# Two layers of local attention and SwiGLU: where staging and the size pass write, and in which order two attention streams run

## The chip, the cores and the metric

The kernel runs on one core of one Trainium2 chip. The metric is the device time of one execution in microseconds (us). Before the change it is 1657.15 us, the median of 18 runs (1651.94 to 1660.99). Engines are named as the profile names them: PE (matrix products; PEld is its weight load), DVE (VectorE), ACT (ScalarE), POOL (GpSimd) and SP (SyncE, which here issues nearly all DMAs).

## The reference, cut to what matters

One sequence of 2048 tokens, D = 1024, 32 heads of 32, F = 3584, in bf16. Two layers share one set of weights:

```
for layer in range(2):
    x = x + A(layernorm(x))     # attention
    x = x + B(layernorm(x))     # SwiGLU
A: q, k, v = split(x @ wqkv)
   each token attends to itself and to the tokens 2, 4, ..., 14 before it (W = 8)
   o = softmax(q . k[those] / sqrt(32)) . v[those];  return o @ wo
B: return (silu(x @ w1) * (x @ w3)) @ w2
```

## The kernel before, in words

**Units.** The tokens are cut into four chunks of 512. A unit is one layer's SwiGLU of one chunk; there are eight (`units`, L88). The stages on PE are: q, k and v of layer 0 for all four chunks (L956 to L973), then the eight units in turn (`b_stage`, L869). After the units 1 to 4 come q, k and v of layer 1 for the chunk that is three units ahead (L982 to L987). Attention runs beside these on DVE, in half chunks of 256 tokens (`halves`, L454).

**q, k, v.** `q_part` (L685) computes one of q, k, v for one chunk, transposed: 8 tiles of 8 matmuls (L699). ACT copies each result (L703) into a staging tile `sgt` of two tiles (pool `stg`, two buffers, L77), and SP stores it to a DRAM tensor `qkv_d` (L710). Attention later loads q, k and v of a half from there (`load_part`, L429). After each pair of tiles `then` may issue further loads (L714).

**Attention on DVE.** `score_steps` (L463) takes a half at a time. It multiplies q by eight shifted k (L478) and folds each product in a tree (L402, L404) into `psm`. PE sums over each head's elements (`gather_heads`, L491), DVE and ACT make the softmax (L508 to L522), and PE spreads it back over the partitions (`spread_heads`, L531), which ACT copies into `At` (L533). `value_steps` (L543) then multiplies `At` by shifted v (L562) and folds it into `oT`. `o_tile` (L633) multiplies `oT` by wo on PE (L649) and DVE adds the result to x (L654). Products of both streams take their buffers from the pool `scr` (three). In the kernel before, the score stream stops after queueing the spreading of half h until `At` of h is there (L540), so that the products of half h+1 begin no earlier than the values of h.

**Order.** The order on PE, DVE, ACT and SP is written out by a planner at build time (`manual_schedule`, L81). It keeps a modelled clock of each engine (`now`), with costs written by hand. `background(until)` (L130) puts steps of four queues, in the order norms, sums, values, scores, on DVE as long as they end before `until`. A step is a triple of cost, earliest time and action; a queue that yields `"blocked"` is passed over. PE's attention products wait in `pe_queue` and are put in when the modelled PE clock is 1.5 us past their due time (L457). `x_at` (L90) holds the modelled times at which the four chunks of x are there, `xnT_at` those of the normalised, transposed chunks. The normalisation has two parts, `norm_stats` (L203, DVE statistics L210) and `norm_apply` (L223), which writes `xn` (three buffers) and issues a transposing DMA on SP (L240).

**Weights.** All weights go through one ring of six slots of 8 KB per partition (pool `wp`). `seq` (L576) lists what the ring holds in order; `load_weight` (L591) fills the next entry, and `release`/`flush` (L622, L626) call it once for each slot that PE has finished with. SP issues these loads in program order with everything else.

**SwiGLU.** The units 0 and 1 (u < TU) work in groups of four tiles of 128 columns: w1 (L898, `pg`), Silu on ACT (L902), w3 (L907, `pu`), product on DVE (L911). A group is 64 matmuls. The columns are taken in two splits of four and three groups, and each split is followed by its w2 products (L924). At the side the units 0 and 1 prepare w1 and w3, one each, for the other six units, which form the products from seven combinations of quarter blocks (`products`, L775, matmuls L793). `prepare` (L758) does this by slots, two for each tile of the group. In slot 2, `measure` (L720) lets ACT take the sum of absolute values of the group's weights, the size pass (L723). In slot 5 a matmul sums it over the partitions (L729), DVE turns it into a scale (L733 to L736), and ACT copies the first half of the group, scaled, into block 0 of `big` (L744). In slot 6 ACT copies the second half into block 1. In slot 7 DVE forms the differences in block 0 (L754) and SP stores the block to `t_d` (L756); in slot 1 of the next group the same follows for block 1.

**The buffer `big`** (L183, 8192 elements of two bytes per partition) is used for several things: in the units 0 and 1 for the blocks 0 (from 0) and 1 (from 4096), and for the size pass's element-wise result, which nobody reads (0 to 4096, `junk`); in the later units for `sums` (0 to 3072) and five snapshots of partial products (`snaps`, 3072 to 8192).

Of the kernel before, what the change touches and what calls it, by code (L numbers as in the profile page):

```python
# [8 lines left out]
BF16 = mybir.dt.bfloat16  # L9
# [8 lines left out]
def kernel(  # L18
# [13 lines left out]
    nc = tc.nc  # L32
    cfg = dict(cfg or {})
    P = 128
# [34 lines left out]
    wp = ctx.enter_context(tc.tile_pool(name="wp", bufs=NW))  # L69
    xnp = ctx.enter_context(tc.tile_pool(name="xn", bufs=3))  # L70
    xtp = ctx.enter_context(tc.tile_pool(name="xnT", bufs=2))
    scr = ctx.enter_context(tc.tile_pool(name="scr", bufs=3))
    wk = ctx.enter_context(tc.tile_pool(name="wk", bufs=1))
    smp = ctx.enter_context(tc.tile_pool(name="smp", bufs=1))
    sgp = ctx.enter_context(tc.tile_pool(name="sg", bufs=5))
    small = ctx.enter_context(tc.tile_pool(name="small", bufs=2))
    stg = ctx.enter_context(tc.tile_pool(name="stg", bufs=2))  # L77
    qkvp = ctx.enter_context(tc.tile_pool(name="qkvp", bufs=1))
    dram = ctx.enter_context(tc.tile_pool(name="dram", bufs=1, space=DRAM))
    psum = ctx.enter_context(tc.tile_pool(name="psum", bufs=8, space=PSUM))  # L80
# [6 lines left out]
    now = dict(pe=23.6, dve=15.0, act=24.5, table=None)  # L87
    units = [(l, c) for l in range(2) for c in range(NCH)]  # L88
    norms = []
    x_at = [12.5, 21.5, 25.0, 28.5]  # L90
    xnT_at, norm_left, qkv_at, oT_at, o_todo = {}, {}, {}, {}, {}

    def pe(n, ready=0.0):
# [129 lines left out]
    def norm_apply(key, c, r):  # L223

        if key not in xnTs:
            xnTs[key] = xtp.tile([P, KT, CH], FP16, name="xnT")
        xnT = xnTs[key]
        mv, sd, ready = moments[key, r]
        rstd = small.tile([P, 2], FP32, name="rstd")

        def apply(i):
            j = 2 * r + i
            if key[0] == "Q" and key[1] == 0:
                xn = hT[:, KT + 2 * j:KT + 2 * j + 2, :].rearrange("p a t -> p (a t)").bitcast(FP16)
            else:
                xn = xnp.tile([P, D], FP16, name="xn")[:]
            nc.vector.tensor_scalar(xn, x_sb[:, c * TPC + j, :], mv[:, i, 0:1], rstd[:, i:i + 1],
                                    op0=ALU.subtract, op1=ALU.mult)
            with hp():
                nc.sync.dma_start_transpose(out=xnT[:, :, j * P:(j + 1) * P], in_=xn)  # L240
            xnT_at[key] = now["dve"] + DMA
            norm_left[key] = norm_left.get(key, TPC) - 1

        yield 0.10, ready, lambda: nc.vector.reciprocal(rstd[:], sd[:])
        for i in range(2):
            yield 0.47, 0.0, lambda: apply(i)

    moments = {}
    sums_of, sums_free = {}, [True]

# [26 lines left out]
    def first_q(ws, loads):  # L277
# [18 lines left out]
        load_tile(3, 0, D, nc.sync)  # L296
        load_weight()
        load_weight()
        for c in range(1, NCH):
            load_x(c)  # L300
        preload = small.tile([P, 1], FP32, name="preload", bufs=1)
        nc.scalar.activation(preload[:], epst[:], ACTF.Sqrt)

# [139 lines left out]
        qks[l, h] = qT, kT, max(now["dve"], qkv_at[l, h // R, 1]) + DMA  # L443

    def load_v(l, h):
        if (l, h) in vs or (l, h // R, 2) not in qkv_at or len(av_done) < len(vs):
            return
        vT = qkvp.tile([P, KT, HALO + TCH], BF16, name="vT")
        load_part(vT, l, 2, h * TCH, True)
        vs[l, h] = vT, max(now["dve"], qkv_at[l, h // R, 2]) + DMA  # L450
# [12 lines left out]
    def score_steps():  # L463

        V = nc.vector
        for g, (l, h) in enumerate(halves):
# [21 lines left out]
            def gather_heads(t):  # L488
# [3 lines left out]
                                     rhs=psm[:, :, a * BLK:(a + 1) * BLK], start=True, stop=True)  # L492
                at["t"] = pe(3, t) + 0.2

            t = now["dve"] + 0.2
            pe_queue.append((t, lambda: gather_heads(t)))
            while "t" not in at:
# [28 lines left out]
            At = Ats[l, h] = wk.tile([P, W, TCH], BF16, name="At")  # L526
            t2 = now["dve"] + 0.2

            def spread_heads(a):
                ps = psum.tile([P, W, BLK], FP32, name="pe", tag="mm")  # L530
                nc.tensor.matmul(ps[:], lhsT=spread[:, a, :], rhs=An[:], start=True, stop=True)  # L531
                r = pe(1, t2)
                nc.scalar.copy(At[:, :, a * BLK:(a + 1) * BLK], ps[:])  # L533
                done = act(0.6, r)
                if a == 3:
                    At_at[l, h] = done

            for a in range(4):
                pe_queue.append((t2, lambda a=a: spread_heads(a)))
            while (l, h) not in At_at:  # L540
                yield "blocked"

    def value_steps():  # L543

# [32 lines left out]
    for u in range(len(units)):  # L577
        for f0, f1 in fsplits:
            if u >= TU:
                groups = [(m, g0 // FG) for g0 in range(f0, f1, FG) for m in range(2)]  # L580
                for i, (m, g) in enumerate(groups):
                    seq += [("early", m, g)] + ([("late", *groups[i - 1])] if i else [])
                seq += [("late", *groups[-1])]
            for g0 in range(f0, f1, FG) if u < TU else ():
                seq += [("w1", g0, min(FG, f1 - g0)), ("w3", g0, min(FG, f1 - g0))]
            seq += [("w2", g0, min(8, f1 - g0), hh) for hh in range(2) for g0 in range(f0, f1, 8)]
        if 1 <= u and u + 3 < len(units):
            seq += [("qkv", which, h) for which in range(3) for h in range(2)]
    w_tiles, due, used = [], [], [0]

    def load_weight(pieces=1):  # L591

        if len(w_tiles) == len(seq):
            return
        kind, i, n, *rest = seq[len(w_tiles)]
        if kind == "qkv":
            w = wp.tile([P, KH, D], BF16, name="wqkv", tag="w")
            step = KH // pieces
            for k0 in range(0, KH, step):
                nc.sync.dma_start(w[:, k0:k0 + step, :],  # L600
                                  wqkv_v[:, n * KH + k0:n * KH + k0 + step, i * D:(i + 1) * D])
        elif kind in ("early", "late"):
            early = kind == "early"
            w = wp.tile([P, 2, 4 if early else 3, KT // 2, P], FP16, name=kind, tag="w")
            v = t_d[i][n][:].rearrange("p a (b k c) -> p a b k c", b=7, k=KT // 2)
            nc.sync.dma_start(w[:], v[:, :, 0:4] if early else v[:, :, 4:7])
        elif kind == "w2":
            w = wp.tile([P, 8, 512], BF16, name="w2t", tag="w")
            nc.sync.dma_start(w[:, 0:n, :], w2_v[:, i:i + n, rest[0] * 512:(rest[0] + 1) * 512])
        else:  # L610
            w = wp.tile([P, KT, FG * P], BF16, name=kind + "t", tag="w")
            v = w1_v if kind == "w1" else w3_v
            nc.sync.dma_start(w[:, :, 0:n * P], v[:, :, i * P:(i + n) * P])
        w_tiles.append(w)
# [7 lines left out]
    def release(n):  # L622

        due.extend([None] * n)
# [60 lines left out]
    def q_part(l, c, which, ws, then=()):  # L685
# [6 lines left out]
            kT = qkvp.tile([P, KT, HALO + TCH], BF16, name="kT")  # L692
            nc.vector.memset(kT[:, :, 0:HALO], 0.0)
        for t0 in range(0, KT, SG):
            sgt = stg.tile([P, SG, CH], BF16, name="sgt")
            for t in range(t0, t0 + SG):
                ps = bank("ps")
                for kk in range(KT):
                    nc.tensor.matmul(ps[:], lhsT=ws[kk // KH][:, kk % KH, t::KT], rhs=xnT[:, kk, :],  # L699
                                     start=(kk == 0), stop=(kk == KT - 1))  # L700
                r = pe(KT, ready)
                background(r)
                nc.scalar.copy(sgt[:, t - t0, :], ps[:])  # L703
                done = act(0.6, r)
                if first:
                    nc.scalar.copy(kT[:, t, HALO:], ps[:, 0:TCH])
                    done = act(0.4)
                if t < t0 + SG - 1:
                    pe_requests(2)
            nc.sync.dma_start(qkv_d[l][which][:, t0:t0 + SG, c * CH:(c + 1) * CH], sgt[:])  # L710
            if first and t0 == SG:
                load_part(qT, 0, 0, 0, False)
            between(False)
            if t0 // SG < len(then) and then[t0 // SG]:  # L714
                then[t0 // SG]()
# [1 line left out]
        if first:  # L717
            qks[0, 0] = qT, kT, done + 0.1

    def measure(m, g, w):  # L720

        junk = big[:, 0:4096].bitcast(BF16).rearrange("p (k c) -> p k c", k=KT)
        nc.scalar.activation(junk, w[:], ACTF.Abs, accum_out=size[:, m, g:g + 1])  # L723
        act(3.7)

    def scales(m, g):
# [28 lines left out]
        dve(1.4, r)  # L755
        nc.sync.dma_start(t_d[m][g][:, a, :], b.rearrange("p b k c -> p (b k c)"))  # L756

    def prepare(u, g, slot, w1t, w3t):  # L758

        w = (w1t, w3t)[u]  # L760
        if slot == 1 and g:
            differences(u, g - 1, 1)
        elif slot == 2:
            measure(u, g, w)
        elif slot == 5:
            scales(u, g)
            copies(u, g, w, 0)
        elif slot == 6:
            copies(u, g, w, 1)
        elif slot == 7:  # L770
            differences(u, g, 0)
            if g == NG - 1:
                differences(u, g, 1)
# [95 lines left out]
    def b_stage(u, hold):  # L869
# [7 lines left out]
        for (f0, f1) in fsplits:  # L877
# [4 lines left out]
                    sums_free[0] = True  # L882
            for g0 in range(f0, f1, FG) if u < TU else ():
                gn = min(FG, f1 - g0)
                w1t, w3t = weight("w1"), weight("w3")
                for fi in range(gn):
                    f = g0 + fi
                    slack = 1.0 if f < f1 - 2 else -0.5
# [12 lines left out]
                    sg = sgp.tile([P, CH], BF16, name="sg")  # L901
                    nc.scalar.activation(sg[:], pg[:], ACTF.Silu)  # L902
                    ts = act(0.6, r, "silu")
                    prepare(u, g0 // FG, 2 * fi, w1t, w3t)
                    pu = bank("pu")
                    for kk in range(KT):
                        nc.tensor.matmul(pu[:], lhsT=w3t[:, kk, fi * P:(fi + 1) * P], rhs=xnT[:, kk, :],  # L907
# [2 lines left out]
                    background(r + slack)  # L910
                    nc.vector.tensor_tensor(hT[:, f - f0, :], sg[:], pu[:], op=ALU.mult)  # L911
                    th = dve(0.64, r)
                    prepare(u, g0 // FG, 2 * fi + 1, w1t, w3t)
                release(2)
            for hh in range(2):
                w2ts = [weight("w2") for g0 in range(f0, f1, 8)]
                for j in range(TPC):
# [38 lines left out]
    for c in range(NCH):  # L956
        for which in range(3):
# [5 lines left out]
            if c == 0 and which == 0:  # L963
                continue
            if c == 0 and which == 1:
                then = (lambda: (load_weight(), load_weight()),)
            if c == 2 and which == 0:
                then = (None, None, lambda: nc.sync.dma_start(wo[:], wo_v))
            q_part(0, c, which, w_tiles[2 * which:2 * which + 2], then)
# [48 lines left out]
```

## Time and profile before

| | |
|---|---|
| time, median of 18 runs | 1657.15 us |
| time of the profiled execution | 1657.59 us |
| its span, first to last instruction | 1655.9 us |
| PE, busy | 1598.7 us |
| DVE, ACT, busy | 1223.2, 643.2 us |
| mean granted clock of PE | 0.981 |
| main DMA queue, share of 16 engines | 70.9% |
| stores of q, k, v (`qkv_d<-sgt`) | 92 of 256 KB, 2.3 us to landing |
| stores of blocks (`t_d<-big`) | 28 of 896 KB, 5.0 us to landing |
| loads of w1 and w3 for the units 0 and 1 | 14 and 14 of 1 MB, 7.0 and 8.8 us |
| size passes (L723) | 14 of 3.6 us on ACT |

The profile is of one execution. "Busy" is the time in which an engine has an instruction running. Lists of waits give the engine and line that stood idle, what ended the idle time, the total, the number of times and the longest. The chain of waits is followed back from the last instruction: at each step to what released it. The granted clock is the share of full speed at which PE was allowed to run.

### The profile page before, as it was taken

To read this page: it belongs to the slowest core of one execution; us is meant where nothing else is said; L and a number is where in the kernel's file an instruction comes from. 1 tells how busy PE (TensorE), PEld (TensorE's weight loads), DVE (VectorE), ACT (ScalarE), POOL (GpSimd) and SP (SyncE) were. 2 spreads that over 40 slices of the span, in tenths; PEclk is the share of its full clock that TensorE was granted. 3 is DMA by queue.
4 is the path that set the end of the run, shared out by engine and by line. 5 is a ranking of instruction groups with operands and counts; after the bars stand their busy time and mean duration, and the time that the engine had idled before them with its cause. 6 is when DMAs were issued, how large, how long until landed. Compare 5 with 4: busy or idle time off the path is not lost.

```text
span 1655.9 us, 24405 instructions
## 1 busy us (share of the span) xinstructions
PE 1598.7 (97%) x9844; PEld 1019.9 (62%) x9844; DVE 1223.2 (74%) x2180; ACT 643.2 (39%) x1000; POOL 3.4 (0%) x16
## 2 busy tenths in 40 slices
PE   9899999989899999999999999999999999999999
PEld 7565534434344468585685856857568577676866
DVE  6697687777786769888788978888769798734423
ACT  4433266354716336150452424514245225232422
POOL 0000000000000000000000000000000000000000
PEclk9999989999899999999999999999999999999999
DMA  9554766658766868776787778867779687677954
GB/s 310 161 135 123 207 192 207 197 187 269 229 196 194 282 198 296 228 246 213 233 264 232 255 221 286 255 207 258 214 251 266 231 274 237 226 248 249 322 181 147
DMA packets 298785, 377.90 MB, mean 228 GB/s; under 512 B 71472, under 2 KB 234672, under 8 KB 298544
## 3 DMA queue, kind: packets, MB, share of 16 engines
q1 hardware_dynamic: 298528, 376.22, 70.9%
q8 instruction: 77, 1.26, 0.3%
q14 instruction: 36, 0.29, 0.1%
q10 hardware_dynamic: 144, 0.13, 0.0%
HBM read 305.53 MB, written 55.05 MB: 218 GB/s over the span
## 4 chain that ended last, share of the span: by engine, by line
PE 75%; DVE 14%; DMA 6%; ACT 4%; issue 1%; SPq 1%; ACTq 0%; DVEq 0%
PE st L793 25%; PE acc L924 22%; PE ps L699 13%; PE po L649 7%; PE pg L898 4%; PE pu L907 3%; DVE st L210 2%; DVE pr L478 2%; ACT big L723 2%; DMA xnT<-xn 2%; DVE pr L402 2%; DMA qkv_d<-sgt 1%; DVE tm L562 1%; DMA t_d<-big 1%; DVE hT L807 1%; DVE tm L402 1%
## 5 line engine op out<-in xcount | busy, mean ns | idle before, releaser
L924 PE MATMUL acc<-w2t,hT 128*128 128x512 bf16 (+1 forms) x1804 | 391.9, 378 | 0.0
L699 PE MATMUL ps<-xnT,wqkv 128*128 128x512 f16 (+1 forms) x1472 | 326.2, 382 | 0.0
L924 PEld LDWEIGHTS <-hT 128*128 128x128 bf16 x1804 | 176.3, 98 | 208.1 <-issue 0.7
L793 PEld LDWEIGHTS <-early 128*128 128x128 f16 x2688 | 263.7, 98 | 40.6 <-issue 3.1
L699 PEld LDWEIGHTS <-wqkv 128*128 128x128 bf16 x1472 | 211.0, 144 | 111.2 <-issue 5.8
L793 PEld LDWEIGHTS <-late 128*128 128x128 f16 x2016 | 197.7, 98 | 35.5 <-issue 10.8
L703 ACT CAST sgt<-ps 128x512 bf16<-128x512 f32 x184 | 104.6, 588 | 271.9 <-PE ps L699 191.9
L562 DVE TENSOR_TENSOR tm<-At,vT 128x2048 bf16<-128x2048 bf16 x128 | 156.0, 1219 | 65.2 <-ACT At L533 65.1
L793 PE MATMUL st<-xnT,late 128*128 128x256 f16 x1344 | 175.9, 274 | 2.7 <-DVE big L841 2.3
L793 PE MATMUL st<-big,early 128*128 128x256 f16 x1344 | 173.7, 274 | 2.6 <-ACT st L819 2.6
L793 PE MATMUL st<-xnT,early 128*128 128x256 f16 x1344 | 165.3, 273 | 0.0
L934 DVE TENSOR_TENSOR x_sb<-x_sb,acc 128x512 bf16<-128x512 bf16 x129 | 87.4, 678 | 105.2 <-PE acc L924 104.3
L478 DVE TENSOR_TENSOR pr<-qT,kT 128x2048 bf16<-128x2048 bf16 x128 | 155.9, 1218 | 5.6 <-DMA qT<-qkv_d 5.6
L402 DVE TENSOR_TENSOR pr<-pr 128x1024 bf16<-128x1024 bf16 (+1 forms) x256 | 137.5, 552 | 0.5
L402 DVE TENSOR_TENSOR tm<-tm 128x1024 bf16<-128x1024 bf16 (+1 forms) x256 | 137.1, 551 | 0.4
L819 ACT COPY st<-st 128x512 f32<-128x512 f32 x84 | 48.4, 576 | 226.0 <-PE st L793 222.9
L898 PE MATMUL pg<-xnT,w1t 128*128 128x512 f16 x448 | 116.8, 408 | 2.2 <-ACT sgt L703 2.2
L649 PE MATMUL po<-wo,oT 128*128 128x512 bf16 x512 | 115.7, 379 | 0.0
L907 PE MATMUL pu<-xnT,w3t 128*128 128x512 f16 x448 | 114.3, 401 | 0.0
L802 ACT ACTIVATE sg<-st,down_scale 128x512 bf16<-128x512 f32 x126 | 86.9, 690 | 37.2 <-PE st L793 36.1
L807 DVE SCALAR_TENSOR_TENSOR hT<-st,down_scale,sg 128x512 bf16<-128x512 f32 x126 | 92.9, 745 | 9.5 <-PE st L793 9.2
L831 DVE TENSOR_TENSOR st<-st,big 128x512 f32<-128x512 f32 x84 | 58.3, 695 | 51.8 <-ACT big L828 51.5
(120 smaller groups left out, 1260.7 us busy)
## 6 DMA issues: line engine op xcount, KB each, us to landing
early<-t_d SPq DMA_DIRECT2D x84, 1024.0 KB, 7.0
late<-t_d SPq DMA_DIRECT2D x84, 768.0 KB, 6.5
w2t<-in_B_w_dram SPq DMA_DIRECT2D x48, 1024.0 KB, 7.6
wqkv<-in_A_wqkv_dram SPq DMA_DIRECT2D x28, 1024.0 KB, 7.7
t_d<-big SPq DMA_DIRECT2D x28, 896.0 KB, 5.0
qkv_d<-sgt SPq DMA_DIRECT2D x92, 256.0 KB, 2.3
w1t<-in_B_w_dram SPq DMA_DIRECT2D x14, 1024.0 KB, 7.0
w3t<-in_B_w_dram SPq DMA_DIRECT2D x14, 1024.0 KB, 8.8
```

Of the source, the lines that this page charges most:

```text
L402: nc.vector.tensor_tensor(b[:, 0:m, :], b[:, 0:m, :], b[:, m:2 * m, :], op=ALU.add)
L478: V.tensor_tensor(pr[:], qT[:], kT[:, :, k0:k0 + TCH], op=ALU.mult)
L562: V.tensor_tensor(tm[:], At[:], win, op=ALU.mult)
L649: nc.tensor.matmul(ps[:], lhsT=oT[:, t, j * P:(j + 1) * P], rhs=wo[:, t, hh * 512:(hh + 1) * 512], start=(t == 0), stop=(t == KT - 1))
L699: nc.tensor.matmul(ps[:], lhsT=ws[kk // KH][:, kk % KH, t::KT], rhs=xnT[:, kk, :], start=(kk == 0), stop=(kk == KT - 1))
L703: nc.scalar.copy(sgt[:, t - t0, :], ps[:])
L793: nc.tensor.matmul(out[:, a, :], lhsT=w[:, a, blk, k, :], rhs=rhs[:, k, :], start=start and a == 0 and k == 0, stop=k == KQ - 1, skip_grou ...
L807: nc.vector.scalar_tensor_tensor(hT[:, f:f + 2, t0:t0 + HT], src, inv, gates[g, q][:], op0=ALU.mult, op1=ALU.mult)
L898: nc.tensor.matmul(pg[:], lhsT=w1t[:, kk, fi * P:(fi + 1) * P], rhs=xnT[:, kk, :], start=(kk == 0), stop=(kk == KT - 1))
L907: nc.tensor.matmul(pu[:], lhsT=w3t[:, kk, fi * P:(fi + 1) * P], rhs=xnT[:, kk, :], start=(kk == 0), stop=(kk == KT - 1))
L924: nc.tensor.matmul(acc[:], lhsT=hT[:, f - f0, j * P:(j + 1) * P], rhs=w2ts[(f - f0) // 8][:, (f - f0) % 8, q0:q0 + step], start=(f == f0), ...
L934: nc.vector.tensor_tensor(xs, xs, acc[:], op=ALU.add)
```

## The change: what it does

Five things are altered together.

- The score stream of half h+1 no longer waits at the end of half h. It waits before its own gather (new lines before L495), so its products can run while `At` of half h is on its way. `spread_heads` binds its tiles when it is made, `load_v` is tied to the order of the halves, and `scr` has four buffers instead of three.
- The pool `stg` is gone. The staging of q, k and v uses pieces of `big`: eight pieces in turn in layer 0, five (those of the snapshots) in layer 1.
- The size pass writes into a slot of the weight ring. Each group of the units 0 and 1 takes three entries of the ring instead of two, the third of which loads nothing.
- The loads of x for the chunks 2 and 3 are issued behind those of v's weights, after the second and third pair of tiles of k of chunk 0, and the planner's times for them are later.
- The planner's times of the transposing DMAs follow one another by at least 1.5 us and are at least 3.0 us after the step, and a normalisation waits in the plan for its buffer of three.

```diff
-    scr = ctx.enter_context(tc.tile_pool(name="scr", bufs=3))
+    scr = ctx.enter_context(tc.tile_pool(name="scr", bufs=4))
-    stg = ctx.enter_context(tc.tile_pool(name="stg", bufs=2))
-    x_at = [12.5, 21.5, 25.0, 28.5]
+    x_at = [12.5, 21.5, 38.0, 44.0]
@@ norm_apply
-            xnT_at[key] = now["dve"] + DMA
+            turned.append(max(now["dve"] + 3.0, turned[-1] + 1.5))
+            xnT_at[key] = turned[-1]
...
-            yield 0.47, 0.0, lambda: apply(i)
-
+            yield 0.47, 0.0 if key[:2] == ("Q", 0) else turned[-3], lambda: apply(i)
+
+    turned = [0.0] * 3
@@ first_q
-        for c in range(1, NCH):
-            load_x(c)
+        load_x(1)
@@ load_v
-        if (l, h) in vs or (l, h // R, 2) not in qkv_at or len(av_done) < len(vs):
+        if (l, h) in vs or (l, h // R, 2) not in qkv_at or len(av_done) < len(vs) or halves[len(vs)] != (l, h):
@@ score_steps
+            while g and halves[g - 1] not in At_at:
+                yield "blocked"
             t = now["dve"] + 0.2
             pe_queue.append((t, lambda: gather_heads(t)))
...
-            def spread_heads(a):
+            def spread_heads(a, At=At, An=An, t2=t2, key=(l, h)):
...
-                    At_at[l, h] = done
+                    At_at[key] = done
             for a in range(4):
-                pe_queue.append((t2, lambda a=a: spread_heads(a)))
-            while (l, h) not in At_at:
-                yield "blocked"
+                pe_queue.append((t2, lambda a=a, f=spread_heads: f(a)))
@@ seq
-                seq += [("w1", g0, min(FG, f1 - g0)), ("w3", g0, min(FG, f1 - g0))]
+                seq += [("w1", g0, min(FG, f1 - g0)), ("w3", g0, min(FG, f1 - g0)), ("junk", 0, 0)]
@@ load_weight
+        elif kind == "junk":
+            w = wp.tile([P, KT, FG * P], BF16, name="junk", tag="w")
@@ q_part
-            sgt = stg.tile([P, SG, CH], BF16, name="sgt")
+            i = (c * 3 + which) * KT // SG + t0 // SG
+            i = 8 - i % 8 if l == 0 else 8 - i % 5
+            sgt = big[:, (i - 1) * SG * CH:i * SG * CH].bitcast(BF16).rearrange("p (a t) -> p a t", a=SG)
...
-            nc.sync.dma_start(qkv_d[l][which][:, t0:t0 + SG, c * CH:(c + 1) * CH], sgt[:])
+            nc.sync.dma_start(qkv_d[l][which][:, t0:t0 + SG, c * CH:(c + 1) * CH], sgt)
@@ measure
-    def measure(m, g, w):
-
-        junk = big[:, 0:4096].bitcast(BF16).rearrange("p (k c) -> p k c", k=KT)
-        nc.scalar.activation(junk, w[:], ACTF.Abs, accum_out=size[:, m, g:g + 1])
+    def measure(m, g, w, junk):
+
+        nc.scalar.activation(junk[:], w[:], ACTF.Abs, accum_out=size[:, m, g:g + 1])
@@ b_stage
-                w1t, w3t = weight("w1"), weight("w3")
+                w1t, w3t, junk = weight("w1"), weight("w3"), weight("junk")
...
-                release(2)
+                release(3)
@@ the stages of layer 0
-                then = (lambda: (load_weight(), load_weight()),)
+                then = (lambda: (load_weight(), load_weight()), lambda: load_x(2), lambda: load_x(3))
```

More of the change, by code (lines that the diff above doesn't have):

```diff
@@ L756, in differences, with prepare @@
         nc.sync.dma_start(t_d[m][g][:, a, :], b.rearrange("p b k c -> p (b k c)"))
-    def prepare(u, g, slot, w1t, w3t):
+    def prepare(u, g, slot, w1t, w3t, junk):
         w = (w1t, w3t)[u]
@@ L763, in prepare @@
         elif slot == 2:
-            measure(u, g, w)
+            measure(u, g, w, junk)
         elif slot == 5:
@@ L903, in b_stage @@
                     ts = act(0.6, r, "silu")
-                    prepare(u, g0 // FG, 2 * fi, w1t, w3t)
+                    prepare(u, g0 // FG, 2 * fi, w1t, w3t, junk)
                     pu = bank("pu")
@@ L912, in b_stage @@
                     th = dve(0.64, r)
-                    prepare(u, g0 // FG, 2 * fi + 1, w1t, w3t)
-                release(2)
+                    prepare(u, g0 // FG, 2 * fi + 1, w1t, w3t, junk)
+                release(3)
             for hh in range(2):
```

## The prediction

> **What bounds the kernel now.** I read the page's first lists, then the waits, then the chain of waits around the worst ones, then the clock by stretches.
>
> The page's busy list and slices:
>
> ```profile
> span 1655.9 us, 24405 instructions
> ...
> PE 1598.7 (97%) x9844; PEld 1019.9 (62%) x9844; DVE 1223.2 (74%) x2180; ACT 643.2 (39%) x1000; POOL 3.4 (0%) x16
> ...
> PEclk9999989999899999999999999999999999999999
> ```
>
> PE is idle for 1655.9 - 1598.7 = 57.2 us. The answer by cores gives a mean granted clock of 0.981, so a further (1 - 0.981) x 1655.9 = 31 us is lost to matmuls at a lowered clock. No change that leaves the matmuls alone can win more than these 88 us. What counts is where PE stands still, not how busy VectorE is. The list of waits (engine and line, what it waited for, total us, times, longest):
>
> ```profile
> ACT sgt L703 <- DMA qkv_d<-sgt: 73.5, 20, 12.4
> ...
> DVE tm L562 <- ACT At L533: 65.1, 13, 10.3
> ...
> PE size L729 <- ACT big L723: 25.1, 8, 4.2
> ...
> ACT big L723 <- DMA t_d<-big: 15.5, 4, 5.0
> ```
>
> The first two are large but are waits of ACT and DVE, which mostly cost PE nothing. The third is PE itself, eight times for 25.1 us, nearly half of its idle time. The chain of waits around one of the eight (start, us, what):
>
> ```profile
> 328.82 1.74 PE pg L898 x8
> ...
> 331.05 4.95 DMA t_d<-big
> ...
> 336.16 3.72 ACT big L723 x2
> ...
> 339.93 0.59 PE size L729 x2
> 340.51 3.44 PE pg L898 x8
> ```
>
> The size pass (L723) writes its throw-away result over the block that the store `t_d<-big` is still reading, so it starts only when that store lands (336.00). PE had nothing left at 335.73 and waits 4.20 us for the sum over partitions (L729). Then eight matmuls take 3.44 us, where the same eight took 1.74 before: half clock. In the trace all eight size passes of this kind start 0.1 to 0.2 us after that store lands. The clock by stretches (length, PE busy, ..., PEclk):
>
> ```profile
> 131.48:138.00 6.52, 4.62 (x22) 2.97 (x23) 1.77 (x3) 2.87 (x6) 0.00 (x0) 1.00 0.65 203
> ...
> 335.73:347.00 11.27, 7.08 (x20) 2.89 (x21) 7.55 (x17) 9.56 (x12) 0.00 (x0) 0.70 0.77 256
> ...
> 414.06:422.10 8.04, 5.63 (x21) 2.36 (x21) 4.59 (x10) 6.13 (x9) 0.00 (x0) 0.79 0.77 271
> ```
>
> The second stretch loses 0.30 x 11.27 = 3.4 us, the third 0.21 x 8.04 = 1.7, the first (a gap of 1.90 us) nothing.
>
> **The change part by part.**
>
> *Size pass into a ring slot: what it removes.* The eight PE gaps are 3.85, 4.08, 4.20, 2.41, 3.32, 1.77, 2.28 and 3.22 us, 25.1 in all. Each is followed by a half-clock stretch, four of 3.41 us and four of 6.83: 41.0 us at half speed lose 20.5. The Trainium skill (TensorE: Matmul & The Clock Gate, Part 1) says that the clock halves after at least one idle window of about 3.4 us. By it only the three gaps above 3.4 us would have cost clock, 8.5 us, and the sum would be 33.6. The rows show lowered stretches after gaps of 1.77 to 3.32 too, so I take 25.1 + 20.5 = 45.6. Does the stall go wholly? Without the wait the pass would start when the activation before it ends (331.18 in the shown case), take 3.7 us and end at 334.9, before PE runs dry at 335.73. The same sum for the other seven leaves 0.6 to 0.9 us of slack. So it goes, but the slack is thin.
>
> *What is late next, first: block 1.* The copies into the second block (the second four L744) would start about 15 us after the group's start, but that block's previous store lands late, as two weight loads are queued ahead of it: issued at 229.80, 9.6 us to landing, so at 239.4, 18.4 us into a group that began at 221.0. They are hidden today because the size pass made them late anyway (239.91). Freed, they wait 3 us, end at 21, and delay the next group's size pass by 1 to 2 us. Three or four groups follow one another without an output tile of attention between to hide that: I take 3.5 us, ends 0 and 8.
>
> *Second: the ring.* It keeps six slots, but a third of those of a group now hold no weights, so weights are loaded one group (13.8 us) ahead instead of two. The row: with the group from 221.0, w1 and w3 are issued 5.8 and 6.3 us into it (behind the store of block 0 on SP), and take 7.6 and 10.0 us. They land at 13.4 and 16.3; PE needs them at 13.8 and 15.5. So w1 just arrives and w3 is 0.8 late; today it has 13.8 us more. The worst flush (w2 at 268.8 and 270.7, landed 277.6 and 281.0) would be 1.3 and 3 us late. Eight loads have no attention tile as cover; summing them this way gives 6 us, ends 0 (stores leave earlier) and 30 (SP held 3 us longer each time). The skill (DMA: Bandwidth & Descriptors, Measured) gives 6.15 us for 1 MB; by it both weights would come in time and the cost would be nothing. The row is the loaded queue of this kernel, so I take 6. A gap near 2 us sometimes trips the clock (1.77 did, 1.90 did not): two trips of 1.7, 3.4 us. Net of the size pass: 45.6 - 3.5 - 6 - 3.4 = 32.7 us gained.
>
> *Staging in the sums' buffer.* Eight stages deep in layer 0 and five in layer 1, instead of two. ACT's 73.5 us of waiting for staging stores mostly go. On PE they show at two places: a gap of 2.17 us at 203.1 with its 1.7 us of clock, and, less surely, 1.78 us at 621.0 where ACT's copy of the first product is late after such waits. Saved: 3.9 + 1.8 = 5.7. It adds a wait: the first snapshots of layer 1's products are written over stages still being stored. Queued behind such a copy on ACT is the next copy of a product, and PE waits for that about 2.6 us later. By the order of the slots the snapshot needed first was staged at least two stages (3.5 us each) before the end, except at the last boundary, where the final stage (copy to landing 2 to 3 us) meets the third product. I take 0, ends 0 and 4.
>
> *Overlap of the two streams.* Products of the next half fill VectorE while the weights of attention travel through PE and ACT: that fills the 65.1 us above. VectorE's order changes, its work doesn't. The fourth scratch buffer adds no wait, since only VectorE, in order, uses these. PE waits for VectorE's attention in four gaps: 4.84 at 60.5, 1.90 at 131.5, 2.17 at 788.3, 4.13 at 1195.3 (clock: 3.4, 0, 0, 1.7). The last two are attention being late, 8.0 us with clock; some of it goes, but a newly packed VectorE may be late elsewhere. Ends -8 and +8; I take -3. The transposes' times in the planner only reorder VectorE, which today waits 9.8 us for them in three places, none of which stops PE: 0.
>
> *Late x loads.* They leave SP at 9.9 to 12.7 us, where nobody waits behind them, and come after the query load for the first half (41.2). Behind them on SP stand only staging stores, which the deeper staging covers. But the statistics of chunks 2 and 3 (29.7 to 41.0 us, 11.3 us of VectorE) run today while VectorE has nothing else: it then idles 5.6 us for the query load that lands at 46.5. Moved, they stand before and among the first score products. A transfer of 1 MB issued at about 42 behind that 0.5 MB (5.3 us) lands near 48 to 50. So the first scores end some 13 us later (65.2 to about 78). The planner knows of 10 of these and places PE's use later by as much; the remaining 3 lengthen the gap of 4.84 us, with a little clock: +4, ends -8 (the planner's times now fit) and +10. The 10 us are caught up before the output tiles at 150 us, as VectorE is busy only 13.9 of 25 us between 125 and 150. v's weights are gated by the first staging store (28.5), not by x, so they gain nothing.
>
> *Sum.* -32.7 - 5.7 + 0 - 3 + 4 = -37.4. The profiled execution took 1657.6 (span 1655.9 and 1.7 around it), so 1620.2; the median of the runs shown is 0.4 lower, so 1620.
>
> **The rivals.**
>
> *All covered.* The stores and loads leave SP earlier once ACT isn't stopped, neither ring nor block 1 is late, and the start costs nothing: -45.6 - 5.7 - 3 = -54, about 1603. For it: each t_d store is late today partly because of the stall. Against it: the group from 205.3 had no stall, and its loads still left 5.8 us into the next.
>
> *The waits come back as others.* Ring and block 1 at twice my sizes with their clock (26), the start at its upper end (10), VectorE later on PE's path (+5): -51 + 26 + 10 + 5 = -10 to -20, about 1642. For it: every margin above is under 1 us.
>
> *Ring starvation, slower than before.* SP issues in order. If the store ahead of the weights waits for a VectorE fuller than today, the eight uncovered loads slip together. A gap of 3.32 us with its 6.83 us half-clock stretch costs 6.7. Eight make 54, more than the 51 gained. It decides from about 3.2 us of lateness per load, against under 1 us by the rows; at 4 us, eight cost about 60, giving 1665.
>
> *The pass still waits*, since its slot's old readers or the slot's turn hold it as the store did: only the 5.7 and the start's +4 remain, 1656. Against it: slots are reused in order, after PE has left the group.
>
> **How the numbers follow.** Forecast 1620 (own range 1609 to 1633): 0.60. All covered, 1603: 0.17. Waits as others, 1642: 0.15. Still waiting, 1656: 0.03. Starvation, 1665: 0.05. A measurement of this kernel tells 0.2% (3 us) from no change. Faster: 0.60 + 0.17 + 0.15 = 0.92; same 0.03; slower 0.05. The range runs from the all-covered case less its own spread, 1598, to the third case, 1644.
>
> **What would show it.** The size matmul (L729 now) no longer idle for the size pass; the size pass following the gate activation of its own group at once. If the ring is short, PE gaps ahead of the first gate or w2 matmul of a group, ended by a weight DMA. If block 1 is, ACT's second four copies wait about 3 us for `t_d<-big`. Staging: no ACT wait for `qkv_d`. Start: VectorE waiting for x past 45 us and a gap at the first gather of 7 to 8 us. A mean clock near 0.99. The prediction is wrong if PE idle falls by less than 10 us, or if idle moves to the products (L793), for which I expect nothing.

## The result, and the profile after

The changed kernel takes 1632.16 us (median of 8 runs; 1629.83 to 1634.55) against 1658.59 for the kernel before, run beside it. The ratio is 0.9847, 95% interval 0.9832 to 0.9863: some 25 us faster. The forecast was 37 us, 1620. The measured time lies at the upper end of the leading case's own range, 1609 to 1633.

The page of the kernel after (its lines are numbered two to four higher than before):

```profile
span 1630.4 us, 24503 instructions
...
PE 1583.5 (97%) x9844; PEld 1014.8 (62%) x9844; DVE 1221.0 (75%) x2180; ACT 648.1 (40%) x1002; POOL 3.4 (0%) x16
```

PE's idle time fell from 57.2 to 1630.4 - 1583.5 = 46.9 us, by 10.3. The mean granted clock rose from 0.981 to 0.991: the clock records of the two traces hold 61.4 and 27.7 us at half clock, and half of the difference is 17 us. Together that is 27 us, 1.6 more than the difference of the spans (25.5); these 1.6 us are not explained. PE's own waits in the kernel after (engine and line, what it waited for, total us, times, longest):

```profile
PE st L796 <- DVE st L834: 9.5, 8, 3.5
PE L L491 <- DVE vT L431: 8.9, 1, 8.9
PE L L491 <- DVE psm L404: 7.5, 2, 4.8
PE size L732 <- ACT junk L726: 5.3, 4, 3.6
PE st L796 <- DVE big L844: 3.3, 9, 1.2
PE pu L910 <- DMA w3t<-in_B_w_dram: 2.0, 3, 1.0
...
PE acc L927 <- DMA w2t<-in_B_w_dram: 0.9, 1, 0.9
```

The size sum, first of PE's waits before with 25.1 us, is now fourth. Products and attention's gathers stand above it. In the kernel before they followed it:

```profile
PE L L491 <- DVE psm L404: 6.6, 3, 4.1
PE st L793 <- DVE st L831: 5.5, 3, 2.6
PE L L491 <- DVE vT L431: 4.8, 1, 4.8
```

The books of both traces, each gap of PE with half the length of the half-clock stretch that belongs to it (us, idle + clock):

| where PE stood | before | after | forecast difference | measured |
|---|---|---|---|---|
| size sums | 25.1 + 20.5 | 5.3 + 1.7 | -42.1 | -38.6 |
| weights late (ring) | 0 | 3.2 + 0 | +9.4 | +3.2 |
| staging, at 203 us | 2.2 + 1.7 | 0 | -3.9 | -3.9 |
| first gather | 4.8 + 3.4 | 8.9 + 5.1 | +4 | +5.8 |
| later gathers and spreads | 8.5 + 1.7 | 9.4 + 1.7 | -3 | +0.9 |
| products (L793, now L796) | 10.3 + 3.4 | 14.3 + 5.1 | -1.8 | +5.7 |
| start, rest | 2.7 | 2.6 | 0 | -0.1 |

The measured column sums to -27.0, the forecast one to -37.4. Some stretches of half clock begin while PE still stands, and that part costs nothing beside the gap: 6.2 us of half clock before and 6.7 after. This hardly moves the sum, but without it four rows read -36.7 (size sums), +4.8 (first gather), +0.6 (later gathers) and +4.9 (products).

Three lines of the list of all waits of the kernel after show where the time went, two of VectorE and one of ACT:

```profile
DVE pr L478 <- DMA kT<-qkv_d: 53.2, 7, 26.5
...
DVE st L209 <- DMA x_sb<-in_A_x_dram: 26.2, 2, 19.9
ACT big L747 <- DMA t_d<-big: 21.2, 8, 7.0
```

VectorE stands 53.2 us for k, where it stood 5.6 for q before and not at all for k: attention has caught up with the stage that computes k. The chain of waits into the products' gap at 1197.8 (start, us, what) begins at such a load and goes on over score products on VectorE to the step that PE waits for, at 1200.89:

```profile
1177.62 9.19 DMA kT<-qkv_d
...
1200.23 0.62 DVE st L834
```

VectorE stands 19.9 us for the late x. ACT waits 21.2 us for a block's store, where it was 4.0 for these copies before. The stretches from the start of the first gather's gap and of the products' gap at 1197.8 (length, PE busy, ..., PEclk):

```profile
72.44:88.00 15.56, 6.64 (x21) 2.81 (x22) 10.40 (x24) 2.94 (x4) 0.00 (x0) 0.67 0.66 149
...
1197.84:1207.00 9.16, 6.11 (x30) 4.21 (x30) 9.16 (x17) 2.67 (x5) 0.00 (x0) 0.63 0.25 77
```

They hold 0.33 x 15.56 = 5.1 and 0.37 x 9.16 = 3.4 us of lost clock beside gaps of 8.9 and 3.1 us. The clock went down at 76.9 and 1199.9, before the gaps ended, so what PE lost beside the gaps is 2.9 us each.

What is left of the size stalls is one gap, 3.6 us at 427.0. The chain of waits into it (start, us, what):

```profile
410.96 9.39 DMA t_d<-big
...
420.44 1.48 ACT big L747 x3
...
423.01 1.28 ACT L214
...
424.62 1.28 ACT L905
...
425.92 1.08 ACT sg L905 x2
427.00 0.94 ACT junk L726
...
430.65 0.38 PE size L732 x2
```

The store of block 1 takes 9.39 us to land behind two weight loads, ACT's copies wait for it, two table loads follow (a normalisation's square root, then Silu again), and the size pass begins at 426.9. An estimate without that wait is 422, as the gate product of its slot ends on PE at 421.9. This is the wait the prediction put next in line.

### The profile page after: what moved, and what is told of

Its sections match the earlier page's. It is cut to its first block, busy times and chain, and to the rows that moved or that the text cites. A ratio compares the mean times of both kernels' runs of the same rounds, so it can differ in the third digit from the quotient of the medians.

```text
span 1630.4 us, 24503 instructions
## 1 busy us (share of the span) xinstructions
PE 1583.5 (97%) x9844; PEld 1014.8 (62%) x9844; DVE 1221.0 (75%) x2180; ACT 648.1 (40%) x1002; POOL 3.4 (0%) x16
## 4 chain that ended last, share of the span: by engine, by line
PE 70%; DVE 18%; DMA 8%; ACT 2%; issue 1%; SPq 1%; DVEq 0%; ACTq 0%
PE st L796 24%; PE acc L927 21%; PE ps L703 11%; PE po L651 6%; PE pu L910 3%; PE pg L901 3%; DVE tm L562 3%; DVE pr L478 3%; DMA xnT<-xn 2%; DVE tm L402 2%; DVE pr L402 2%; DMA t_d<-big 2%; DMA kT<-qkv_d 2%; DVE st L209 2%; DVE hT L810 1%
## 5 line engine op out<-in xcount | busy, mean ns | idle before, releaser
L796 PEld LDWEIGHTS <-early 128*128 128x128 f16 x2688 | 263.7, 98 | 41.5 <-issue 2.0
L796 PEld LDWEIGHTS <-late 128*128 128x128 f16 x2016 | 197.7, 98 | 42.8 <-issue 18.1
L707 ACT CAST big<-ps 128x512 bf16<-128x512 f32 x184 | 106.2, 586 | 226.6 <-PE ps L703 221.5
L478 DVE TENSOR_TENSOR pr<-qT,kT 128x2048 bf16<-128x2048 bf16 x128 | 155.8, 1217 | 53.2 <-DMA kT<-qkv_d 53.2
L796 PE MATMUL st<-xnT,late 128*128 128x256 f16 x1344 | 175.3, 274 | 3.6 <-DVE big L844 3.3
L796 PE MATMUL st<-big,early 128*128 128x256 f16 x1344 | 174.0, 274 | 1.2 <-ACT st L822 1.2
L796 PE MATMUL st<-xnT,early 128*128 128x256 f16 x1344 | 166.4, 273 | 0.0
L910 PE MATMUL pu<-xnT,w3t 128*128 128x512 f16 x448 | 106.9, 382 | 2.4 <-DMA w3t<-in_B_w_dram 2.0
L901 PE MATMUL pg<-xnT,w1t 128*128 128x512 f16 x448 | 106.5, 381 | 0.3 <-DMA w1t<-in_B_w_dram 0.3
L810 DVE SCALAR_TENSOR_TENSOR hT<-st,down_scale,sg 128x512 bf16<-128x512 f32 x126 | 92.9, 745 | 12.1 <-PE st L796 12.0
```

What stands on the lines that cost most here:

```text
L478: V.tensor_tensor(pr[:], qT[:], kT[:, :, k0:k0 + TCH], op=ALU.mult)
L796: nc.tensor.matmul(out[:, a, :], lhsT=w[:, a, blk, k, :], rhs=rhs[:, k, :], start=start and a == 0 and k == 0, stop=k == KQ - 1, skip_grou ...
L810: nc.vector.scalar_tensor_tensor(hT[:, f:f + 2, t0:t0 + HT], src, inv, gates[g, q][:], op0=ALU.mult, op1=ALU.mult)
L901: nc.tensor.matmul(pg[:], lhsT=w1t[:, kk, fi * P:(fi + 1) * P], rhs=xnT[:, kk, :], start=(kk == 0), stop=(kk == KT - 1))
```

## The experiments

All ratios are to the kernel before, run beside each kernel. Where two kernels were not run beside each other, their difference in us is the difference of their ratios times 1655.

| run | median us | before, beside it | ratio | 95% interval |
|---|---|---|---|---|
| after | 1632.16 | 1658.59 | 0.9847 | 0.9832 to 0.9863 |
| e1 size pass in the ring only | 1630.52 | 1655.84 | 0.9851 | 0.9829 to 0.9874 |
| e2 after without that | 1657.13 | 1655.84 | 1.0002 | 0.9988 to 1.0015 |
| e3 after, x and its times early | 1639.70 | 1655.84 | 0.9907 | 0.9892 to 0.9922 |
| e4 after without overlap | 1643.54 | 1655.84 | 0.9928 | 0.9914 to 0.9943 |
| e5 after, x early, its times late | 1621.51 | 1654.89 | 0.9798 | 0.9776 to 0.9821 |
| e6 size pass in the ring, and staging | 1626.37 | 1654.89 | 0.9827 | 0.9805 to 0.9850 |
| e7 as e6, ring whole | 1613.76 | 1654.89 | 0.9749 | 0.9728 to 0.9770 |
| e8 after, q and k by GpSimd | 1631.41 | 1654.89 | 0.9855 | 0.9834 to 0.9876 |
| e9 as e5, k later in the planner | 1616.51 | 1654.61 | 0.9764 | 0.9748 to 0.9781 |
| e10 as e5, without overlap | 1630.57 | 1654.61 | 0.9852 | 0.9837 to 0.9867 |
| e11 as e7, first half later in the planner | 1628.76 | 1654.61 | 0.9843 | 0.9828 to 0.9858 |
| e12 after, transposes' times as before | 1638.45 | 1654.00 | 0.9898 | 0.9868 to 0.9927 |

**e1, the size pass alone.** The kernel before with the change's lines for `junk` (ring entry, `measure`, `prepare`, `release(3)`), cut:

```diff
-                seq += [("w1", ...), ("w3", ...)]
+                seq += [("w1", ...), ("w3", ...), ("junk", 0, 0)]
-        nc.scalar.activation(junk, w[:], ACTF.Abs, ...)      # junk = big[:, 0:4096]
+        nc.scalar.activation(junk[:], w[:], ACTF.Abs, ...)   # junk = weight("junk")
```

> The kernel before with one part of the change: the size pass writes into a third ring entry of each group; everything else as before. Theory 1 (the size pass's wait for the block store was the main cost, ring and block 1 cost little): PE's idle time for the size sums falls from 25.1 us to about 5, half-clock stretches by some 35 us, PE idles some 3 us for weight loads; 33 to 38 us faster than before, about 1622. Theory 2 (the other parts bring the gain, the smaller ring eats what the size pass wins): within 10 us of before, with PE gaps of 2 us and more ahead of the first gate, up or w2 product of a group.

Measured: 0.9851, about 25 us, as much as the whole change. The size sums fall to 4.1 us of gaps. But PE waits 10.6 us for weights, more than theory 1's 3 or my forecast of 6, and in one place 4.7 us with 3.4 of clock. Theory 1 holds in kind, and the ring's price is mis-sized; of theory 2 the one gap above 2 us is there, but not the small gain.

**e2, everything but the size pass.** The same lines undone in the kernel after.

> The kernel after with the size pass put back over block 0 and two ring entries for each group. Theory 1: the eight stalls come back, 33 to 40 us slower than after, about 1668, so slower than before too, as the rest of the change loses a few us. Theory 2: only some 10 us slower than after, about 1642.

Measured: 1.0002, so the other four parts together bring nothing here; undoing one part costs 26 us. PE's wait for the size sums is back (25.7 us, seven times). Theory 2 falls; theory 1 is right in kind, but its 33 to 40 us were too many.

**e3, x as before.**

```diff
-    x_at = [12.5, 21.5, 38.0, 44.0]
+    x_at = [12.5, 21.5, 25.0, 28.5]
-        load_x(1)
+        for c in range(1, NCH):
+            load_x(c)
...
-                then = (..., lambda: load_x(2), lambda: load_x(3))
+                then = (lambda: (load_weight(), load_weight()),)
```

> The kernel after with the loads of x for the chunks 2 and 3, and the planner's times for them, as they were before. Theory 1 (VectorE stands idle for x and then does 11 us of statistics ahead of the first scores, and the planner is too early by the difference): the gap at the first gather falls from 8.9 us to about 5 and its half-clock stretch from 10.2 to 6.8, 5 to 6 us faster than after, about 1626. Theory 2 (the moved loads relieve the start, the longer gap has another cause): the gap stays near 9 us, time within 1 us of after or slower.

Measured: 1639.70, some 10 us slower than after. The start did as theory 1 said (gap 5.2 us, half clock 6.8), but the total fell the other way. PE's waits in this run:

```profile
PE size L733 <- ACT junk L727: 16.0, 5, 5.7
...
PE acc L928 <- DMA w2t<-in_B_w_dram: 5.0, 1, 5.0
```

The softmaxes in the units 0 and 1 now start 24 to 28 us earlier (261.7, 347.5 and 438.8 us against 289.3, 374.1 and 462.4). In the three longest gaps at the size sums (4.5, 5.7 and 4.9 us) the chain of waits has such a softmax, with two table loads of 1.28 us each, on ACT just ahead of the size pass. So the edit has two effects, the loads and a new plan, and e5 takes them apart.

**e4, no overlap.** In the kernel after the score stream stops at the end of each half as before:

```diff
-            while g and halves[g - 1] not in At_at:
-                yield "blocked"
...
+            while (l, h) not in At_at:
+                yield "blocked"
```

> The kernel after with the score stream stopping at the end of each half until its At is there, as before. Theory 1 (overlap only brings attention up to the point where k isn't there yet; VectorE then stands for k up to 26 us and is late for the products): the waits of 12, 10 and 26 us for k shrink to a few us, PE's gaps in the products fall by 3 to 5 us plus clock, 3 to 8 us faster than after. Theory 2 (filling VectorE's idle time helps PE): attention is late again at forced output tiles, 4 to 10 us slower than after.

Measured: 0.9928, 13 us slower than after. An output tile is forced when the plan has PE take it whether or not VectorE is done with its values. PE waits 12.9 us for such tiles at 348 us; of the half clock that goes with them most lies inside these gaps, and 2.4 us more are lost:

```profile
PE po L651 <- DVE oT L404: 12.9, 3, 9.6
...
PE st L796 <- DVE st L834: 5.3, 3, 2.4
```

Theory 2 holds for the time. But the first half of theory 1 came true as well: VectorE's waits for k are gone altogether, and PE's idle time in the products falls from 14.3 to 10.1 us, about what it was before the change. So overlap is what makes VectorE wait for k and come late to the products; with the late planner times it is needed all the same, for the forced tiles.

**e5, x loads early, planner's times late.** The two `load_x` hunks of e3 without the first.

> The kernel after with the x loads of chunks 2 and 3 issued where they were before, but with the planner's later times kept, so that the order on every engine but SP is that of after. Theory 1 (VectorE's 19.9 us wait for x is what makes PE wait at the first gather, and the loss of the run with loads and times both early came from where attention then falls in the later plan): the statistics end at 41 us, the first scores at 67, PE's gap of 8.9 us there and its half-clock stretch go, nothing else changes; 12 to 14 us faster than after, about 1619. Theory 2 (early x loads hold up something else at the start or later): within 3 us of after.

Measured: 0.9798, 8 us faster than after (the spans differ by 11.2); the gap at the first gather is gone and the mean clock is 0.995. Theory 1 holds. The late load shows no benefit of its own, and the late time in the planner is what is worth having (e5 against e3). The size is a little under the 12 to 14 expected, as small gaps grew by a few us.

**e6 and e7, the price of the ring.** e6 is e1 with the staging in `big`. e7 is e6 with two ring entries for each group and the size pass writing to a buffer of its own, of an 8-bit type (cut; the size pass also gets `saturate=False`):

```diff
+    junk_t = const.tile([P, KT, FG * P], mybir.dt.float8e4, name="junk_t")
...
-        junk = big[:, 0:4096].bitcast(BF16).rearrange(...)
+        junk = junk_t[:]
```

> The kernel before with the size pass in the ring and the staging in the sums' buffer, nothing else. Theory 1 (staging saves its two gaps): 2 to 6 us faster than with the size pass in the ring alone, about 1626. Theory 2 (staging is hidden anyway or the snapshots wait for it): equal to that run within 2 us, 1629 to 1633.

> The kernel before with the staging in the sums' buffer and the size pass writing to a buffer of its own (4 KB, an 8-bit type, which nobody reads), so that the ring keeps two entries for each group and weights come two groups ahead. Theory 1 (the smaller ring costs PE some 10 us and 3 of clock in gaps ahead of w3 and w2 products): these gaps go, 8 to 14 us faster than the same with the size pass in the ring, about 1615. Theory 2 (what holds PE is the second block's store and ACT, not the ring): less than 4 us faster, and the gaps move to the size sum.

Measured: 1626.37 and 1613.76, 12.6 us apart, run beside each other. e6 is 4 us better than e1, with overlapping intervals. The gap at 203 us is gone in e6, but in e1 too, where staging is as before: with one weight load fewer ahead of the staging stores on SP, ACT waits 5.0 us there instead of 8.2. What only e6 lacks is a gap of 1.6 us at 592.7, which in e1 leads back over ACT's copies to a staging store. PE's waits in e6:

```profile
PE acc L926 <- DMA w2t<-in_B_w_dram: 7.7, 4, 4.5
...
PE size L731 <- ACT junk L725: 4.3, 2, 3.6
PE pu L909 <- DMA w3t<-in_B_w_dram: 3.0, 3, 1.5
```

and in e7, where no wait for a weight is left:

```profile
PE st L795 <- DVE st L833: 7.7, 3, 4.0
PE L L491 <- DVE psm L404: 6.4, 3, 3.9
PE L L491 <- DVE vT L431: 5.4, 1, 5.4
PE size L731 <- ACT junk_t L725: 5.2, 2, 4.0
```

The 10.7 us of weight waits go, with some 3 of clock. Some 3.6 us come in their place, 2.5 of them in the products and 0.9 at the size sums: theory 1. The chain into e6's longest shows why it is 4.5 us and not one:

```profile
504.90 11.01 DMA t_d<-big
...
515.93 2.57 ACT big L746 x4
...
520.80 6.10 DMA w2t<-in_B_w_dram
...
526.95 3.15 PE acc L926 x7
```

Block 1's store lands late, ACT's copies and VectorE's differences follow, SP stores the block, and only then, in SP's order, comes the w2 load that PE needs.

**e8, q and k by GpSimd.** `load_part(..., nc.gpsimd)` for q and k in `load_qk`.

> The kernel after with the loads of q and k for attention issued by GpSimd instead of SP, so that they don't queue behind weight loads; the order on PE, DVE and ACT is that of after. Theory 1 (VectorE's waits of 12, 10 and 26 us for k make it late for the products that follow): the waits shrink by 3 to 5 us each, the product gaps of 3.5 and 3.1 us with their clock shrink or go, 3 to 8 us faster than after. Theory 2 (the wait is for k to be computed, not for the load, and the products are late for another reason): within 2 us of after, or slower by the other queue's own delay.

Measured: 0.9855, the same as after. VectorE's waits for k are 10.8, 9.5 and 27.1 us, against 12.1, 10.4 and 26.5. So another queue does not shorten them. Theory 2 holds for the time; that the products are late for another reason, its second half, does not follow, as the waits stayed.

**e9, k later in the planner.** e5 with `qkv_at[l, h // R, 1] + 9.0` in `load_qk`.

> The version with x's loads early and the planner's times late, and in the planner q and k of a half come 9 us later after they are computed, which is what the trace shows. Theory 1 (the planner, not the queue, makes VectorE late for the products: it plans score products 10 us before k can be there): the product gaps of 2.9, 1.6 and 3.1 us with their clock go, 4 to 8 us faster than that version's 1621.5. Theory 2 (a new plan is a new draw: gaps of 2 to 5 us come up at other places): within 5 us either way, with other gaps.

Measured: 1616.51, 5 us less than e5, with intervals that just overlap. VectorE still waits 10.5 and 23.2 us for k, having nothing else to do, but PE's waits in the products fall from 14.8 to 9.7 us. The gaps at 988 and 1187 us are gone, and a new one of 4.1 us stands at 1235, where a k load took 9.4 us. So the planner's optimism about k may account for part of the products' loss. How much isn't settled.

**e10, e5 without overlap.** The edit of e4 on e5.

> The version with x's loads early and the planner's times late, with the score stream stopping at each half's end as before. Theory 1 (overlap was needed in the changed kernel only because the late x puts attention behind; with x there in time the forced output tiles of the run without overlap, 12.9 us at 348 us and their clock, find VectorE done): those gaps go, time within 5 us of that version or faster, 1615 to 1622. Theory 2 (overlap is worth some 11 us by itself, as between after and after without overlap): 8 us or more slower than that version, about 1632.

Measured: 0.9852, 9 us slower than e5. Theory 1 falls: the forced tiles wait 12.7 us although x was there in time. The chain into that wait:

```profile
325.25 12.82 DMA t_d<-big
...
338.10 2.56 ACT big L748 x4
...
341.14 0.44 DVE big L758
...
343.68 1.14 DVE tm L563
```

ACT waits 6.7 us for block 1's store, VectorE's differences (L758) stand behind the copies, and the last value products (L563), planned behind these, find PE already waiting. With overlap (e5) PE takes these output tiles without a gap. As in e4, VectorE has no wait for k, and PE's idle time in the products is 10.5 us, against 14.8 in e5.

**e11, the first half later in the planner.** e7 with `qks[0, 0] = qT, kT, done + 7.5`.

> The version with staging in the sums' buffer and a buffer of its own for the size pass, and in the planner the first half's q and k come 7.4 us later (the trace: first score product at 46.6 us, planned at 39). Theory 1 (the gap at the first gather, 5.4 us with 3.4 of clock, is only this misjudged time): it goes, 6 to 9 us faster than 1613.8, about 1606. Theory 2 (a new plan is a new draw): the gap goes, but others of the same sum appear at the size sums or the products, 1610 to 1622.

Measured: 1628.76, 15 us slower than e7. The gap at the first gather is gone, as meant, and forced output tiles (5.1 and 2.3 us), a gather of 4.9 and their clock came instead: theory 2.

**e12, the transposes' times.** The `turned` lines of the kernel after undone.

> The kernel after with the planner's times of the transposing DMAs as before (2.5 us after the step, no waiting for a free buffer in the plan). Theory 1 (forecast: VectorE's waits for a transpose cost PE nothing, so the planner's new times bring nothing): within 2 us of after. Theory 2 (they keep VectorE from standing in front of the products or a forced gather): 3 to 8 us slower, with more of VectorE's waits for the transpose ahead of a PE gap. Theory 3 (a new plan is a new draw): faster by as much.

Measured: 0.9898, some 8 us slower by the ratio and 6 by the medians. PE's waits for scores rise from 7.5 to 14.3 us. Theory 2; my forecast of 0 for this part was wrong.

## Why the prediction was right in kind and its gain 12 us too large

**The cause stands.** The size pass's wait for the store cost PE the eight gaps and their half clock. Taking it away is the gain (e1 alone, e2 by its absence). The eight gaps shrank to 5.3 + 1.7 us, against 3.5 allowed for block 1. One slip is in the sum ahead of it: of the 41.0 us at half clock 3.8 lie inside the gaps, so the eight cost PE 43.7 us rather than 45.6. The other four parts, forecast at -4.7 us, brought nothing on top of the size pass by the runs (e1 against after).

**Row against rule.** Three of the eight gaps were longer than the 3.4 us that the Trainium skill names (TensorE: Matmul & The Clock Gate, Part 1), but all eight came with half clock. As the gaps went, the clock lost at the size sums fell by 18.8 us (16.9 without the parts inside gaps), where the prediction's estimate from the page had 8.5. The rows were the better guide.

**The ring.** Forecast 6 + 3.4 us. In the kernel after it is 3.2 us of gaps and no clock; with the size pass alone it is 10.6 + 3.4. The same ring costs more than three times as much under another plan. The mechanism was as written: loads one group ahead, behind a block's store on SP. e7 shows what it is worth when removed: 12.6 us. The estimate from the Trainium skill's 6.15 us for 1 MB (DMA: Bandwidth & Descriptors, Measured; for a load issued from GpSimd, without the time of issuing it) was a cost of nothing. The w2 load of e6 did take 6.10 us from issue to landing, but was issued late.

**Staging.** Forecast -5.7. The -3.9 at 203 us is seen, but it isn't shown to be the staging's: the gap is gone with the ring entry alone (e1). For the -1.8 in the products speaks the gap that e6 lacks and e1 has. The time of the two differs by 4 us, within their intervals.

**The start.** Forecast +4, measured +5.8: x landed at 49.3, in the range named, and the gap is 8.9 us, where 7 to 8 was written. Its clock stretch of 10.2 us was also longer than thought, though 4.4 us of it lie inside the gap.

**The step that failed: the overlap of the two streams.** The prediction took -3 for gathers and spreads, and in the products expected no new idle time, only the staging's -1.8. They measured +0.9 and +5.7, 11 us off. That is nearly the whole miss; the other terms (size sums 3.5 and start 1.8 too low, ring 6.2 too high) nearly cancel, which is luck. The prediction had named two signs of being wrong. One came: idle moved to the products, from 10.3 to 14.3 us. The other was missed narrowly: PE's idle time fell by 10.3 us, and less than 10 would have spoken against it.

Two things were wrong. First, VectorE's filled idle time brought attention forward to where k doesn't exist yet; VectorE then stands up to 26.5 us with work of the products queued behind, and is 3 us late for them, twice with lowered clock. The runs show this: without overlap (e4, e10) the waits for k are gone and the products' idle time is back at 10.1 and 10.5 us. That the planner's time of k is part of it rests on e9, which is not beyond the intervals. Second, I added the parts as if each had a price of its own. Overlap is worth 9 to 13 us beside the late planner times of x (e10 against e5, e4 against after), far more than the -3. With early times the kernel with overlap (e3) is 13 us slower than e6, which lacks overlap and also the transposes' times; a run with only overlap taken from e3 was not made.

**The rivals.** Starvation didn't come, and neither did a pass that still waits. The third ("waits come back as others", 1642) has its share: some 15 of the 38.6 us gained on the size sums were given back, most of it in the products and at the start.

The best versions found are e7 (1613.8, 16 us better than after by the ratios) and e9 (1616.5). They were not joined: each spends the 4 KB per partition of the staging pool that is gone, e9 on the fourth scratch buffer and e7 on the size pass's own. Whether both fit is not shown.

## What to carry to other kernels

A result that nobody reads still needs a place, and here it cost most where that place was a buffer with a slow reader. Where memory allows, give it a small buffer of its own rather than a slot of the prefetch ring: here the ring was worth 12.6 us. In a kernel with a written-out order, price an edit by the waits it takes away, and its new order as a draw of some 10 us either way: keep the planner's times apart from the issue order when testing (e3 against e5), since each can hide the other.

## What was not expected of the hardware

- ACT's size pass takes 3.61 us with an 8-bit output as with a 16-bit one, so the smaller buffer cost nothing in time.
- The half-clock stretch at a gap has no fixed length, and the gap's length does not give it. In the kernel after it is 3.4 us at gaps of 3.5, 3.6 and 4.8 us, 6.8 at one of 3.1, 10.2 at one of 8.9, and there is none at one of 2.8. Up to the last microsecond of the spans, where some are cut off, the stretches of both kernels are one, two or three times 3.41 us, and some begin before the gap ends.
- Loads of k through GpSimd's queue took 8.0 us to land (median, e8), against 7.3 through SP in the kernel after: the second queue gave no faster way past 1 MB weight loads.
